# Moving the loads and DMA transposes of six units apart, and the work that waits for them, in a fused retention and MLP kernel

## The chip, the core and the metric

One core of a Trainium2 chip runs the whole kernel. The metric is the device time of one execution in microseconds (us). Engines are named as in the profile: PE is the matrix engine (its weight loads are shown apart as PEld), DVE the vector engine, ACT the scalar engine, POOL the general engine, SP the engine that here only issues DMAs. Each engine runs its own queue of instructions in order, and engines wait for one another with semaphores.

## What is computed

```python
# q, k, v: (8, 8, 576, 64)
scores = scale * np.matmul(q, k.transpose(0, 1, 3, 2))
gamma = 1.0 - 2.0 ** (-5.0 - np.arange(H, dtype=np.float32))
Dmat = np.where(rel >= 0, gamma[:, None, None] ** rel[None, :, :], 0.0)   # rel = i - j
x = np.matmul(scores * Dmat[None], v)       # then heads side by side: 4608 x 512
h = x @ w_in                                # 512 x 2048
out = (h * (1.0 / (1.0 + np.exp(-1.702 * h)))) @ w_out   # 2048 x 512
```

A retention layer (attention without softmax, with a decay that depends on the head) over 8 batches of 576 tokens, and a two-layer MLP with a quick gelu over all 4608 tokens.

## The kernel before

**Units and chunks.** The 4608 tokens are 36 units of 128. Four units are a chunk, and the 9 chunks go through the MLP one after the other. Chunk 0 is units 0 to 3, chunk 1 units 4 to 7, chunk 2 units 8 to 11, and so on. While PE works on the MLP of chunk c, the retention of chunk c + 1 is strewn in between.

**What a unit needs.** `load` issues three DMAs on POOL: k and q into a bf16 tile `kqn` (line 214), v into `vn` (line 227). There are 12 such tiles, so unit 12 uses the tiles of unit 0. Scores need k and q with the head dimension on the partitions. For units 0 to 7 PE transposes them (line 344) and ACT or DVE copies them out of PSUM. From unit 8 on one DMA, issued on SP, transposes `kqn` into `kqT` (`dma_transpose`, line 371). There are 8 tiles `kqT`, with the keys T0 to T7: unit 8 uses T0, unit 13 uses T5.

**Retention in pairs.** Pair j is units 2j and 2j + 1. Unit 8 is one of the units that hold the last 64 tokens of two batches and carry no state on.
- `scale_v` (DVE, line 336) multiplies v with its decay, into `vp`.
- `ahead(j)` puts on PE the scores of the pair (line 477, reading `kqT`) and its contribution to the running state (line 406).
- `ahead_out(j)` puts on DVE the masking of the scores (line 486, into `pm`) and the running sums of the state (lines 419 and 421, into `stm`), and then `state_cast` on ACT, the cast of the sums to bf16 (line 430, into `kv`).
- `block(j)` puts on PE the part that comes from earlier tokens (`inter`, line 461, reading `kv` and `kqT`) and that from the unit itself (`values`, line 499), with `ahead(j + 1)` between two halves of the latter; on DVE it scales the results into `xT` (line 524) and runs `ahead_out(j + 1)`.

**The MLP.** `up` multiplies `xT` with 128 columns of w_in (four matmuls) into PSUM bank A or B by turns, and ACT takes gelu of it into `gT` (line 541). Chunks 0 and 1 do part of it in halves (`up_group`, lines 550 and 555). `down(c, r, s)` multiplies `gT` of unit r of the chunk with w_out, in four quarters s of four matmuls (line 562). `finish_unit` copies the result out (ACT, line 572) and stores it by a DMA on SP (line 578).

**What sets the order.** The order of each engine's queue is the order in which the Python functions call `op`. The class `Program` derives the waits: for each key that an operation reads or writes it waits for the last writer, and for a write also for the readers. A DMA has a semaphore of its own per tile. `load(u, after=[...])` and `dma_transpose` are ordered among one another only through these keys and through their place in POOL's and SP's queue. `lead_in` writes chunk 0, `steady` the others.

Around the change:
- Loads 0 to 11 are issued in `lead_in`. Loads 12 and 13 read key T3, so they wait for the transpose of unit 11.
- Transposes 8 and 9 stand behind the store of the second unit of chunk 0, 10 to 13 behind the fourth.
- The loads of chunk c's far units read the key of the last transpose before them: those of 14 to 17 wait for the transpose of unit 13.
- In chunk 1 the pair of units 8 and 9 has its scores after `up_group` number 11 of 16 and its cast after number 14; `block(4)` stands after down(1, 0, 0), `block(5)` after down(1, 2, 0).

Of the kernel before, what the change touches and what calls it, by code (L numbers as in the profile page):

```python
# [15 lines left out]
NU = (B * S) // P  # L16
# [142 lines left out]
def bass_retnet_parallel__then__act_gelu_quick_kernel(  # L159
# [10 lines left out]
    with es:  # L170
# [195 lines left out]
                transpose_copy(u, 0, bk, ck)  # L366
            transpose_copy(u, 1, bq, cq)

        def dma_transpose(u):
            sl = u % NLD  # L370
            op("sp", lambda e: e.dma_start_transpose(  # L371
                kqT[u % NQT].ap(), kqn[sl].ap().rearrange("p t h d -> p (t h d)")),
               reads=[f"kq{sl}_0", f"kq{sl}_1"], writes=[f"T{u % NQT}_0", f"T{u % NQT}_1"],
               dma=f"d_T{u % NQT}")

        def key(u, a):
# [280 lines left out]
        def lead_in():  # L657
            load_kq0(0)
            load_kq0(1)
            iota_small()  # L660
            iota_large()
            load_v(0)
            load(1)
            load_win(0)
            load(2)
            load_win(1)
            load(3)
            load_win(2)
            load_win(3)
            for i in range(4):  # L670
                load_wout(i)
            for u in range(4, NPE + 4):
                load(u)
            op("dve", lambda e: e.memset(gT[1][:, 0, :], 0.0), writes=["warm"])
            warm(7)
            setup_dve()
            setup_dve2()
            setup_vfac()
            for a in range(4):
                gq_first(a)  # L680
            g_powers()
            gelu_table()
            cast_kq0(0, "dve")
            cast_kq0(1, "dve")
            transpose_pe(0, 0, "E")
            transpose_copy(0, 0, "E", "dve")
            warm(1)
            transpose_pe(0, 1, "B")
            transpose_copy(0, 1, "B", "act")
            warm(4)  # L690
            scores(0)
            scale_v(0)
            gq_next(1)
            scores_out(0, 1, 0)
            scores_out(0, 1, 1)
            state_half(0, 0)
            warm(2)
            transpose_pe(1, 0, "E")
            transpose_copy(1, 0, "E", "act")
            warm(1)  # L700
            transpose_pe(1, 1, "B")
            transpose_copy(1, 1, "B", "act")
            gq_next(2)
            block1(0)
            scale_v(1)
            warm(2)
            scores(1)
            warm(3)
            state_half(1, 0)
            scores_out(1, 1, 0)  # L710
            scores_out(1, 1, 1)
            warm(3)
            block1(1)
            warm(4)
            up_group(0, 0, 2, 0, 2, "A")
            transpose_pe(2, 0, "E")
            transpose_copy(2, 0, "E", "dve")
            up_group(0, 2, 2, 0, 2, "B")
            transpose_pe(2, 1, "E")
            transpose_copy(2, 1, "E", "act")  # L720
            warm(2)
            scale_v(2)
            scores(2)
            state_half(2, 0)
            gq_next(3)
            scores_out(2, 1, 0)
            scores_out(2, 1, 1)
            warm(2)
            up_group(0, 4, 2, 0, 2, "A")
            block1(2)  # L730
            up_group(0, 6, 2, 0, 2, "B")
            transpose_pe(3, 0, "E")
            transpose_copy(3, 0, "E", "dve")
            up_group(0, 0, 4, 2, 3, "A")
            transpose_pe(3, 1, "E")
            transpose_copy(3, 1, "E", "act")
            scale_v(3)
            up_group(0, 4, 4, 2, 3, "B")
            state_half(3, 0)
            scores(3)  # L740
            scores_out(3, 1, 0)
            scores_out(3, 1, 1)
            up_group(0, 8, 2, 0, 2, "A")
            block1(3)
            up_group(0, 10, 2, 0, 2, "B")
            up_group(0, 8, 2, 2, 4, "A")
            up_group(0, 10, 2, 2, 4, "B")
            up_group(0, 0, 4, 3, 4, "A")
            up_group(0, 4, 4, 3, 4, "B")
            gq_next(4)  # L750
            gq_next(5)
            for f in range(12, NF):
                up(0, f)
            def after8():
                ahead(2)
                scores_out(4, 2, 0)
                scores_out(4, 2, 1)

            def after9():
                transposes(6, "B", "B")  # L760
                for u in (4, 5):
                    state_sum(u, 0)
                    state_sum(u, 1)
                scale_v(6)
                scale_v(7)
                state_cast(4, 6)

            work = {
                (0, 3): lambda: (scale_v(4), transposes(4, "E", "E")),
                (1, 3): lambda: (scale_v(5), transposes(5, "C", "C")),  # L770
                (2, 0): after8,
                (2, 1): after9,
                (2, 3): lambda: transposes(7, "C", "C"),
                (3, 0): lambda: block(2, cast=False),
            }
            for r, s in [(i % 2, i // 2) for i in range(8)] + [(i // 4, i % 4) for i in range(8, NF)]:
                down(0, r, s, "AB"[r % 2])
                if (r, s) in work:
                    work[r, s]()
                if s == 3:  # L780
                    finish_unit(0, r, "AB"[r % 2])
                    if r == 1:
                        dma_transpose(8)
                        dma_transpose(9)

        def steady():
            for c in range(1, NCH):
                if c == 1:
                    dma_transpose(10)
                    dma_transpose(11)  # L790
                    for u in (12, 13):
                        load(u, after=["T3_0"])
                for u in range(4 * c + 6, min(4 * c + 10, NU)):
                    if c > 1 or u > 11:
                        dma_transpose(u)
                for u in range(4 * c + 10, 4 * c + 14):
                    load(u, after=[f"T{(4 * c + 9) % NQT}_0"])
                if c == 1:
                    for i in range(16):
                        f0, lo = 2 * (i % 8), 2 * (i // 8)  # L800
                        up_group(1, f0, 2, lo, lo + 2, "AB"[i % 2])
                        if i == 1:
                            state_cast(6, 8)
                        if i == 3:
                            block(3, lambda: None)
                            scale_v(8)
                            scale_v(9)
                        if i == 8:
                            scale_v(10)
                            scale_v(11)  # L810
                        if i == 11:
                            ahead(4)
                            ahead_out(4, False)
                        if i == 14:
                            state_cast(8, 10)
                else:
                    for f in range(NF):
                        up(c, f)
                        if f % 4 == 0:
                            m = 4 * c + 6 + f // 4  # L820
                            if m < NU:
                                scale_v(m)
                if c == NCH - 1:
                    for r in (3, 0, 1):
                        b = "AB"[(r + 1) % 2]
                        for s in range(4):
                            down(c, r, s, b)
                        finish_unit(c, r, b)
                    for n0, b, cp in ((0, "B", "act"), (256, "A", "dve")):
                        for s in range(4):  # L830
                            down(c, 2, s, b, n0, n0 + 256)
                        finish_unit(c, 2, b, n0=n0, n1=n0 + 256, cp=cp)
                    break
                for r in range(4):
                    for s in range(4):
                        down(c, r, s, "AB"[r % 2])
                        if c == 1 and r == 1 and s == 0:
                            scale_v(12)
                            scale_v(13)
                        if s == 0 and r % 2 == 0:  # L840
                            j = 2 * c + 2 + r // 2
                            if 2 * j < NU:
                                block(j)
                    finish_unit(c, r, "AB"[r % 2])

        lead_in()
        steady()
# [60 lines left out]
```

## Time and profile before

| | us |
|---|---|
| median of 3 runs (300.06, 301.92, 302.25) | 301.92 |
| span of the profiled execution | 299.2 |
| POOL idle before the loads of unit 12 | 21.7 |
| first and last issue of a transpose for units 8 to 13 | 49.98, 77 |
| loads of unit 12 issued from | 68.48 |
| loads of unit 14 issued from | 80.83 |
| scores of units 8 and 9 on PE, from | 65.99 |
| block(4) on PE, from | 70.96 |
| block(5) on PE, from | 79.13 |
| PE begins the up projections of chunk 2 | 87.2 |

A line of the profile's table of groups names the line of the code, the engine, the operation, the tile written and the tiles read, the count, the busy time and mean of one, and the idle time of the engine just before with what ended most of it. In a timeline the columns are start, duration, then the same names; a bracket at the end gives the idle time before and what ended it. "issue" there means that the engine waited for nothing that the profile shows. SP's rows are the instructions that issue DMAs, not the transfers; the table of DMA issues gives the time from issue to landing.

### The profile page before, as it was taken

How to read it: one execution, taken by the hardware profiler on the slowest of the kernel's cores; microseconds unless marked ns; L12 is line 12 of the kernel's file. 1: busy time of each engine (PE TensorE's matmuls, PEld its weight loads, DVE VectorE, ACT ScalarE, POOL GpSimd, SP SyncE). 2: the span in 40 equal slices, each digit the busy share in tenths (PEclk: the TensorE clock that was granted, in tenths of full speed). 3: DMA queues.
4: the chain of work that ended last, by engine and by line, in shares of the span. 5: the costliest groups of instructions: out<-in, count | busy, mean ns of one | idle time of the engine just before them, and what ended most of it. 6: DMA issues, size and time to landing. Idle time of an engine off the chain costs nothing.

```text
span 299.2 us, 7913 instructions
## 1 busy us (share of the span) xinstructions
PE 289.9 (97%) x3583; PEld 141.5 (47%) x3583; DVE 98.7 (33%) x198; ACT 135.1 (45%) x236; POOL 108.2 (36%) x137
## 2 busy tenths in 40 slices
PE   7989998989999999999999999999999999999996
PEld 2568354766443454345334443444344534443344
DVE  6553037435541245114800580048005700410000
ACT  8346344653246423642365226522662266216611
POOL 9999482007194085076009500940080000000000
PEclk9999999999999999999999999999999999999999
DMA  9999999999999999999379927991995160110021
GB/s 165 166 209 206 207 219 247 148 161 104 192 169 176 137 110 227 210 112 186 122 175 99 210 58 200 123 195 41 194 103 89 40 142 0 37 72 35 0 71 71
DMA packets 117234, 40.63 MB, mean 136 GB/s; under 512 B 106064, under 2 KB 110416, under 8 KB 117200
## 3 DMA queue, kind: packets, MB, share of 16 engines
q0 software_dynamic: 80160, 22.81, 67.2%
q1 hardware_dynamic: 37040, 17.31, 27.7%
q8 instruction: 28, 0.46, 0.7%
q14 instruction: 6, 0.05, 0.1%
HBM read 36.70 MB, written 9.44 MB: 154 GB/s over the span
## 4 chain that ended last, share of the span: by engine, by line
PE 67%; DMA 15%; POOL 14%; issue 2%; SPq 1%; ACT 0%; DVE 0%; POOLq 0%
PE psA L562 18%; PE psB L562 17%; PE psA L536 14%; PE psB L536 14%; DMA kqn<-in_q_dram 8%; POOL kqn L214 7%; DMA kqT<-kqn 7%; POOL vn L227 4%; POOL w_in_sb L252 2%; PE psX L461 1%; POOL w_out_sb L259 1%; PE psC L477 1%; PE psK L406 1%; PE psX L499 1%; SPq L371 1%
## 5 line engine op out<-in xcount | busy, mean ns | idle before, releaser
L214 POOL DMA_DIRECT2D kqn<-in_k_dram x39 | 35.0, 907 | 113.2 <-DMA kqT<-kqn 110.5
L562 PE MATMUL psA<-w_out_sb,gT 128*128 128x512 bf16 (+1 forms) x304 | 70.3, 374 | 0.0
L562 PE MATMUL psB<-w_out_sb,gT 128*128 128x512 bf16 (+1 forms) x288 | 64.4, 373 | 1.4 <-issue 1.4
L536 PE MATMUL psA<-xT,w_in_sb 128*128 128x512 bf16 x232 | 59.5, 379 | 0.0
L536 PE MATMUL psB<-xT,w_in_sb 128*128 128x512 bf16 x232 | 59.5, 379 | 0.0
L430 ACT ACTIVATE kv<-stm 128x1024 bf16<-128x1024 f32 (+1 forms) x16 | 15.2, 949 | 71.9 <-DVE stm L421 71.9
L524 DVE TENSOR_TENSOR xT<-psX,gq 128x512 bf16<-128x512 f32 x16 | 11.1, 692 | 107.1 <-PE psX L499 107.1
L562 PEld LDWEIGHTS psB<-w_out_sb,gT 128*128 128x128 bf16 x288 | 27.7, 98 | 33.8 <-issue 2.4
L562 PEld LDWEIGHTS psA<-w_out_sb,gT 128*128 128x128 bf16 x304 | 27.6, 98 | 31.3 <-ACT gT L541 2.5
L541 ACT ACTIVATE gT<-psA 128x512 bf16<-128x512 f32 x58 | 34.6, 597 | 15.5 <-PE psA L536 15.5
L541 ACT ACTIVATE gT<-psB 128x512 bf16<-128x512 f32 x58 | 34.6, 597 | 15.4 <-PE psB L536 15.4
L227 POOL DMA_DIRECT2D vn<-in_v_dram x40 | 36.9, 930 | 3.2 <-issue 3.1
L336 DVE TENSOR_TENSOR vp<-vn,vfac 128x512 bf16<-128x512 f32 x36 | 23.7, 687 | 43.4 <-DMA vn<-in_v_dram 43.4
L214 POOL DMA_DIRECT2D kqn<-in_q_dram x39 | 35.3, 917 | 0.0
L536 PEld LDWEIGHTS psA<-xT,w_in_sb 128*128 128x128 bf16 x232 | 18.6, 97 | 31.2 <-ACT gT L541 15.9
L536 PEld LDWEIGHTS psB<-xT,w_in_sb 128*128 128x128 bf16 x232 | 18.0, 97 | 32.1 <-ACT gT L541 15.9
L572 ACT ACTIVATE osb<-psB 128x512 f32<-128x512 f32 (+1 forms) x18 | 10.5, 586 | 20.6 <-PE psB L562 20.6
L550 PE MATMUL psB<-xT,w_in_sb 128*128 128x256 bf16 (+1 forms) x128 | 14.7, 259 | 1.2 <-issue 1.2
L550 PE MATMUL psA<-xT,w_in_sb 128*128 128x256 bf16 (+1 forms) x128 | 14.6, 260 | 0.3 <-DMA w_in_sb<-in_moe_w_in_dram 0.3
L572 ACT ACTIVATE osb<-psA 128x512 f32<-128x512 f32 x18 | 10.5, 584 | 9.6 <-PE psA L562 9.6
L486 DVE TENSOR_TENSOR pm<-psC,mask 128x512 bf16<-128x512 f32 (+1 forms) x20 | 12.6, 630 | 5.0 <-PE psD L477 5.0
L486 DVE TENSOR_TENSOR pm<-psD,mask 128x512 bf16<-128x512 f32 (+1 forms) x20 | 12.6, 628 | 0.0
(67 smaller groups left out, 257.2 us busy)
## 6 DMA issues: line engine op xcount, KB each, us to landing
vn<-in_v_dram POOLq DMA_DIRECT2D x32, 256.0 KB, 5.8
out_dram<-osb SPq DMA_DIRECT2D x31, 256.0 KB, 2.7
kqn<-in_k_dram POOLq DMA_DIRECT2D x31, 128.0 KB, 4.8
kqn<-in_q_dram POOLq DMA_DIRECT2D x31, 128.0 KB, 5.5
w_in_sb<-in_moe_w_in_dram POOLq DMA_DIRECT2D x8, 256.0 KB, 8.9
w_out_sb<-in_moe_w_out_dram POOLq DMA_DIRECT2D x4, 512.0 KB, 16.6
out_dram<-osb SPq DMA_DIRECT2D x10, 128.0 KB, 2.8
vn<-in_v_dram POOLq DMA_DIRECT2D x8, 128.0 KB, 7.1
```

Of the source, the lines that this page charges most:

```text
L214: e.dma_start(kqn[sl][p0 : p0 + n, which, :, :], src[b, :, s0 : s0 + n, :].rearrange("h p d -> p h d"),)
L227: e.dma_start(vn[sl][p0 : p0 + n, :, :], v[b, :, s0 : s0 + n, :].rearrange("h p d -> p h d"))
L252: op("pool", lambda e: [e.dma_start(w_in_sb[64 * pb : 64 * pb + 64, :, 512 * i : 512 * i + 512], moe_w_in[256 * pb : 256 * pb + 256, 512 * ...
L336: op(eng, lambda e: e.tensor_tensor(vp[u % NVP].ap(), vn[sl].ap(), vfac[:, ty, :, None].to_broadcast([P, H, DH]), ALU.mult), reads=[f"vn{s ...
L430: op("act", lambda e: e.activation(kv[:, i0 % NKV : i0 % NKV + n, :, :], stm[:, i0 % 8 : i0 % 8 + n, :, :], AF.Copy), reads=[f"stm{(i0 + i ...
L486: op("dve", lambda e: e.tensor_tensor(pm[(u0 // 2) % 2][hh][:, c0:c1].rearrange("p (a i) -> p a i", i=64), ps32(SB[hh])[:, c0:c1].rearrang ...
L524: op("dve", lambda e: e.tensor_tensor(xT[ch % 2][:, slice(hh, 4, 2), P * jj : P * jj + 2 * P].rearrange("p g (u t) -> p u g t", u=2), ps32 ...
L536: op("pe", lambda e, a=a: e.matmul(bank[b][:, n0:n1], w_in_sb[:, a, P * f : P * f + P], xT[c % 2][:, a, n0:n1], start=(a == 0), stop=(a == ...
L541: op("act", lambda e: e.activation(gT[c % 2][:, f, n0:n1], bank[b][:, n0:n1], AF.Gelu_apprx_sigmoid), reads=[b], writes=[f"g{c % 2}_{f}_{j ...
L550: op("pe", lambda e, a=a, f=f, i=i: e.matmul(bank[b][:, n * i : n * i + n], w_in_sb[:, a, P * f : P * f + P], xT[c % 2][:, a, P * lo : P * ...
L562: op("pe", lambda e, f=f: e.matmul(bank[b][:, 0 : n1 - n0], gT[c % 2][:, f, P * r : P * r + P], w_out_sb[:, f, n0:n1], start=(f == 0), sto ...
L572: op("act", lambda e: e.activation(dst, src, AF.Copy), reads=[b], writes=[f"osb{i}_{n0}"])
```

## The change

Loads 12 and 13 are put right behind load 11, without a wait for a transpose. The six transposes of units 8 to 13 follow on SP, behind the four stores of chunk 0; each reads the key vn1, whose last writer is the load of v of unit 13, so that the first of them waits for it. With this loads and transposes, which were mixed, come in two groups. The loads of units 14 to 17 wait for the transpose of unit 13 as before.

As the transposes come later, what reads them is put later. The scores of units 8 and 9 with all that `ahead_out` has, the cast too, go after down(1, 0, 0). `block(4)` goes after down(1, 1, 0), `block(5)` after down(1, 2, 2). The cast of units 12 and 13 goes from `block(5)` to the end of chunk 1, behind the copy of its last unit. `scale_v` of 12 and 13 keeps its place in the code and comes ahead of `block(4)`'s work on DVE now. The other chunks are as they were.

```diff
-        def dma_transpose(u):
+        def dma_transpose(u, after=()):
...
-               reads=[f"kq{sl}_0", f"kq{sl}_1"], writes=[f"T{u % NQT}_0", f"T{u % NQT}_1"],
+               reads=[f"kq{sl}_0", f"kq{sl}_1", *after], writes=[f"T{u % NQT}_0", f"T{u % NQT}_1"],
...
                     finish_unit(0, r, "AB"[r % 2])
-                    if r == 1:
-                        dma_transpose(8)
-                        dma_transpose(9)
...
                 if c == 1:
-                    dma_transpose(10)
-                    dma_transpose(11)
                     for u in (12, 13):
-                        load(u, after=["T3_0"])
-                for u in range(4 * c + 6, min(4 * c + 10, NU)):
-                    if c > 1 or u > 11:
+                        load(u)
+                    for u in range(8, 14):
+                        dma_transpose(u, ["vn1"])
+                if c > 1:
+                    for u in range(4 * c + 6, min(4 * c + 10, NU)):
                         dma_transpose(u)
...
-                        if i == 11:
-                            ahead(4)
-                            ahead_out(4, False)
-                        if i == 14:
-                            state_cast(8, 10)
...
-                        if s == 0 and r % 2 == 0:
+                        if c == 1 and (r, s) == (0, 0):
+                            ahead(4)
+                            ahead_out(4)
+                        if (r, s) in (((1, 0), (2, 2)) if c == 1 else ((0, 0), (2, 0))):
                             j = 2 * c + 2 + r // 2
                             if 2 * j < NU:
-                                block(j)
+                                block(j, cast=j != 5)
                     finish_unit(c, r, "AB"[r % 2])
+                    if c == 1 and r == 3:
+                        state_cast(12, 14)
```

## The prediction

> **What bounds the kernel now.** I read the page's totals first, then the waits of TensorE (PE) between 40 and 135 us, then the instructions behind them in the timelines of PE, SP, DVE and ACT.
>
> ```profile
> PE 289.9 (97%) x3583; PEld 141.5 (47%) x3583; DVE 98.7 (33%) x198; ACT 135.1 (45%) x236; POOL 108.2 (36%) x137
> ...
> q8 instruction: 28, 0.46, 0.7%
> ```
>
> PE is busy 289.9 of 299.2 us; the other engines are below half. So PE's own order sets the end, and only about 9.3 us of idle PE can be won at all, some 2.7 of them after its last matmul and some 2.7 in the first 20 us, which no edit touches. Who holds PE up in the middle:
>
> ```profile
> PE psB L550 <- issue: 1.2, 1, 1.2
> PE psB L562 <- issue: 0.9, 1, 0.9
> PE psC L477 <- DMA kqT<-kqn: 0.5, 1, 0.5
> PE psC L344 <- DMA kqn<-in_q_dram: 0.3, 1, 0.3
> PE psC L477 <- ACT kqT L354: 0.3, 1, 0.3
> ```
>
> The columns are who waited, for what: us in total, times, longest. Only the third line is a wait for a DMA transpose. The two longest are "issue": nothing in the profile released them. In PE's timeline they, their relative at 145 us and the wait for the transposes are
>
> ```profile
> 51.90 1.25 PE L562 MATMUL psB<-w_out_sb,gT 128*128 128x512 bf16 x5 [0.86 <-issue]
> ...
> 61.75 0.81 PE L550 MATMUL psB<-xT,w_in_sb 128*128 128x256 bf16 x6 [1.25 <-issue]
> ...
> 80.48 0.21 PE L477 MATMUL psC<-kqT 64*64 64x64 bf16 x1 [0.51 <-DMA kqT<-kqn]
> ...
> 145.29 3.19 PE L562 MATMUL psB<-w_out_sb,gT 128*128 128x512 bf16 x14 [0.51 <-issue]
> ```
>
> The view by stretches counts 730 matmuls started before the first "issue" gap, 857 before the second, 2009 before the third. The distances are 127 and 1152 = 9 x 128. The q8 line has 28 packets in 0.46 MB, and 2 x 3583 matmuls and weight loads over 28 packets make 256 instructions, or 128 matmuls, for each. I take these gaps as PE waiting for its next block of instructions, which comes by DMA. That is an inference from the counts. The gap at 61.75 ends 9.9 us after the gap at 51.90, as long as the DMA transposes of that stretch took. In SP's timeline and the table of DMA issues (issues 51.5 to 55.5 us; then 149 to 151 us, where no load is under way):
>
> ```profile
> 49.98 5.37 SPq L371 DMA_TRANSPOSE kqT<-kqn  x2
> ...
> 149.58 5.36 SPq L371 DMA_TRANSPOSE kqT<-kqn  x4
> ```
>
> ```profile
> kqT<-kqn SPq DMA_TRANSPOSE x1, 11.3
> ...
> kqT<-kqn SPq DMA_TRANSPOSE x2, 2.8
> ```
>
> A transpose beside queued loads lands after 11.3 us, one alone after 2.8, and alone they follow one another every 5.36 / 4 = 1.34 us.
>
> **What the skill says.** The Trainium skill, "DMA: Bandwidth & Descriptors", section "Issuing engines are not separate DMA queues", says that DMAs from all issuing engines share 16 DMA engines and interleave. The trace agrees: 11.3 against 2.8 us. Its section "Queues, rings and completion order" says that each DMA engine goes round its queues packet by packet. That fits instructions being late behind transposes; no view shows the order of packets. Its section "Rules for kernel authors" says that a transpose next to ordinary DMAs needs nothing. That is about correctness; in time the neighbourhood costs, as above. No page that I read bears on the wait for PE's instructions.
>
> **The change part by part.**
>
> *Loads 12 and 13 no longer wait for the transpose of 11.* Before, POOL idles 21.7 us and issues them at 68.48. Now they follow load 11, from 46.8 to 52 us. Units land every 2.5 us when little is between them: v of unit 9 at 40.62 + 12.4 = 53.0, of unit 10 at 55.5. Unit 11 came only at 63.8 (DVE's wait for v ends there), with three transposes among the loads. Without them I carry 2.5 us on: unit 11 at 58, 12 at 60.5, 13 at 63. The other bound is 5 us each (the slower steps later in the trace, v of 16 to 17: 96.3 to 102.8, have transposes among them): 70.5. I take 63.5.
>
> *Six transposes behind all loads* (the wait on vn1 is the load of v 13). SP's stores of chunk 0 come before them in its queue and are out by 56.6, and the next store is due only at 78, so nothing else is held on SP. From 63.5 at 1.34 us each and 2.8 us to land: 8 and 9 by 67.7, 10 and 11 by 70.4, 12 and 13 by 73.0. Before, 8 landed at 61.3, 11 at 68.1, 13 at 80.4. The loads of 14 to 17, which wait for 13, start near 73 instead of 80.8.
>
> *Scores of 8 and 9 (ahead(4)) later.* Before they ran at 65.99 to 66.50 inside the up projections; now after the first quarter of down(1,0), at 70.0 + 0.86 - 0.5 = 70.4, or 69.1 if the 1.25 us gap is gone. The transposes are there at 67.7: no wait, margin 1.4. The matmuls are the same ones at another place, and the number of interruptions of the large matmuls is the same: nothing. The cast of unit 9's state has to be ready for block(4). In the trace DVE ends the last sum 2.65 us after the scores begin, and the cast takes 0.62: 73.7 against block(4) at 74.4. Nothing.
>
> *Blocks 4 and 5.* They move from (0,0) and (2,0) to (1,0) and (2,2), six quarters apart instead of eight. In the trace block(4) starts at 70.96 and its cast of two states ends at 77.54, 6.58 us later. The next block comes 1.16 + 6 x 0.863 = 6.34, with the switch some 6.4 us later. So its second group waits **+0.2** us (0 to 0.4).
>
> *Cast of 12 and 13 behind the last copy of chunk 1.* ACT then has the copy, the cast and the first gelu in a row:
>
> ```profile
> 85.36 1.06 ACT L430 ACTIVATE kv<-stm 128x1024 bf16<-128x1024 f32 x1 [6.38 <-DVE stm L421]
> 86.32 0.58 ACT L572 ACTIVATE osb<-psA 128x512 f32<-128x512 f32 x1
> 87.38 0.60 ACT L572 ACTIVATE osb<-psB 128x512 f32<-128x512 f32 x1 [0.48 <-PE psB L562]
> 88.24 0.60 ACT L541 ACTIVATE gT<-psA 128x512 bf16<-128x512 f32 x1 [0.27 <-PE psA L536]
> ```
>
> Copy to cast 0.5, cast to gelu 0.96 (85.36 to 86.32), gelu 0.60: bank A is free 2.1 us after the end of down(1,3). PE wants it for the third up group after 2 x 0.863 = 1.73. **+0.4** us (0 to 0.6), once, as gelu's 0.60 is below the 0.86 of a group.
>
> *What goes.* The wait at 80.48 (0.51) and that for the transpose of unit 17 near 102.7 (0.10): **-0.6**. The gap at 61.75: its instructions were asked for after 51.9, and from there to 63.5 no transpose is under way now. With loads alone in the queue a block needs no more than about 4 us (the gap at 51.9 ended some 4 us after the fast run of small matmuls at 48 us), and there are 9: **-1.25** (0 to -1.4). The gap at 51.9 lies among the same loads; I leave it. The next blocks of instructions come while six transposes run, 63.5 to 73; I add **+0.2** for a late transpose or block (0 to 1.5).
>
> Sum: -0.6 - 1.25 + 0.2 + 0.4 + 0.2 = -1.05. From 301.92 that is **300.9 us**.
>
> **The rivals.** *No gain*, 302.0 us: the gap stays or moves to a block fetched beside the six transposes, so +0.6 stands against -0.6: 301.92 + 0.0 to 0.2. For it: the origin of the gaps is inferred. Against it: both large ones fall where DMA is fullest. *All goes*, 298.7 us: the gaps at 51.9 (0.86) and 145 (0.51) vanish too and the two ACT waits are hidden: 301.92 - 0.61 - 1.25 - 0.86 - 0.51. For it: every later load starts some 7 us earlier, and the runs of before differ by 2.2 us, as waits at the edge would make them. Against it: the first gap precedes the first edit that acts. *A new wait at ahead(4)*, 306 us: the six transposes hang on the last of the loads. At 5 us a unit v 13 lands at 70.5, 9 at 74.7, and PE stands 4.3 us at 70.4 with all down projections behind it in its queue: 301.9 + 4.3 - 0.6 + 0.6 = 306.2. For it: unit 11 took 8.3 us. Against it: that was with transposes among the loads.
>
> **How the numbers follow.** Forecast 0.50, no gain 0.22, all goes 0.18, new wait 0.10. The predicted time is the forecast's, 300.9. The range, 298.8 to 303.3: down nearly to "all goes", up by the bounds of the added waits (1.4 more) and the spread of the three times of before; most of "new wait" is left out. Faster by over 1% (below 298.9) is "all goes" with a little of its misses: 0.17. Slower by over 1% (above 304.9): 0.08. Within: 0.75.
>
> **What would show it.** Right: six transposes 1.34 us apart on SP beginning near 63.5; loads of 14 near 73; no gap of over 0.5 us on PE near 60; no wait for kqT in PE's waits; gelu some 0.4 us late at the start of chunk 2. Wrong: PE waiting at line 477 for kqT near 70 (the transposes are later than I have them), or a gap of "issue" of 1 us at another multiple of 128 matmuls.

## The result: 297.9 us, and where the time went

The changed kernel took **297.9 us** (median of 4 runs, 297.64 to 298.54) against 301.7 us. The ratio is 0.9886, with a 95% interval of 0.9844 to 0.9928. Beside later experiments it was measured twice more: 0.9920 (0.9893 to 0.9947) and 0.9944 (0.9921 to 0.9967). So it is faster by 0.6 to 1.1%, by 2.0 to 3.8 us between the medians, where 1.05 was forecast and 298.8 was the lower end of the range. The kernel before differs more from one set of runs to the next (medians of 300.4 to 301.7 us) than the changed one (297.9 to 298.7), and that makes a good part of the difference between the three ratios.

The page of the changed kernel, the lines that answer to those of before:

```profile
span 295.8 us, 7882 instructions
...
PE 285.1 (96%) x3551; PEld 141.3 (48%) x3583; DVE 97.9 (33%) x198; ACT 135.1 (46%) x236; POOL 108.1 (37%) x137
...
q8 instruction: 28, 0.46, 0.7%
```

The matmuls are the same: 3583 weight loads as before, while 32 records of matmuls are missing from this trace (3551 of 3583). They appear as "issue" waits of 0.16 us and are no gaps. PE's waits between 40 and 135 us, with columns as before:

```profile
PE psA L562 <- issue: 1.0, 6, 0.2
PE psA L536 <- ACT gT L541: 0.4, 1, 0.4
PE psA L562 <- ACT osb L572: 0.4, 1, 0.4
PE psB L562 <- issue: 0.3, 2, 0.2
```

The wait for `kqT` is gone, and so are the gaps of 1.2 and 0.9 us. New is the wait of an up projection for gelu, the second line. SP's timeline has the transposes:

```profile
41.64 11.54 SPq L578 DMA_DIRECT2D out_dram<-osb  x4
63.29 8.55 SPq L371 DMA_TRANSPOSE kqT<-kqn  x6
```

and the table of DMA issues between 63 and 72 us has their time to landing:

```profile
kqT<-kqn SPq DMA_TRANSPOSE x6, 3.1
```

Six transposes from 63.29 on, 8.55 / 6 = 1.43 us each, landing after 3.1 us (median) where those beside loads took 11.3. DVE shows that the loads were early too: its four multiplications of v for units 8 to 11 ran in one go, none waiting for the v of unit 11, which came at 63.8 before.

```profile
57.86 2.49 DVE L336 TENSOR_TENSOR vp<-vn,vfac 128x512 bf16<-128x512 f32 x4
...
70.55 1.28 DVE L336 TENSOR_TENSOR vp<-vn,vfac 128x512 bf16<-128x512 f32 x2
```

**A ledger by stage.** The copies of the results (ACT, line 572) are milestones that both kernels pass in the same order. The table has the time from one to the next, in us, for two traces of the kernel before and three of the changed one.

| stage, from copy to copy | before | before, 2nd | after | after, 2nd | after, 3rd |
|---|---|---|---|---|---|
| start to unit 1 | 42.73 | 42.16 | 42.45 | 42.11 | 43.79 |
| unit 1 to 3 (matmul 730 lies here) | 10.46 | 10.49 | 9.78 | 10.09 | 9.79 |
| unit 3 to 7 (matmul 858, scores and blocks of chunk 1) | 34.19 | 35.73 | 32.13 | 32.33 | 32.14 |
| unit 7 to 11 (late cast, transposes 14 to 17) | 30.29 | 30.88 | 30.61 | 30.61 | 30.62 |
| unit 11 to 15 (matmul 2009) | 30.85 | 30.17 | 30.17 | 30.17 | 30.17 |
| unit 15 to the last | 146.24 | 146.27 | 146.29 | 146.44 | 146.27 |

All the gain lies ahead of unit 15; the last stage differs by no more than 0.2 us. Stage "3 to 7" gives 1.9 to 3.6 us, depending on the pair of traces, and "1 to 3" 0.4 to 0.7. Whether the latter comes from the change is taken up below. The 0.68 us at matmul 2009 is in one trace of before only.

### The profile page after: what moved, and what is told of

Its sections match the earlier page's. It is cut to its first block, busy times and chain, and to the rows that moved or that the text cites. A ratio compares the mean times of both kernels' runs of the same rounds, so it can differ in the third digit from the quotient of the medians.

```text
span 295.8 us, 7882 instructions
## 1 busy us (share of the span) xinstructions
PE 285.1 (96%) x3551; PEld 141.3 (48%) x3583; DVE 97.9 (33%) x198; ACT 135.1 (46%) x236; POOL 108.1 (37%) x137
## 4 chain that ended last, share of the span: by engine, by line
PE 87%; POOL 4%; DMA 3%; ACT 2%; issue 1%; DVE 1%; POOLq 0%; DVEq 0%
PE psA L562 21%; PE psB L562 20%; PE psA L536 17%; PE psB L536 17%; DMA w_in_sb<-in_moe_w_in_dram 3%; PE psA L550 3%; PE psB L550 3%; POOL kqn L214 2%; PE psX L461 2%; POOL vn L227 1%; PE psC L477 1%; POOL w_in_sb L252 1%; PE psX L499 1%; PE psY L499 1%; PE psK L406 1%
## 5 line engine op out<-in xcount | busy, mean ns | idle before, releaser
L214 POOL DMA_DIRECT2D kqn<-in_k_dram x39 | 35.6, 921 | 110.6 <-DMA kqT<-kqn 107.8
L562 PE MATMUL psA<-w_out_sb,gT 128*128 128x512 bf16 (+1 forms) x287 | 66.6, 373 | 2.8 <-issue 2.4
L562 PE MATMUL psB<-w_out_sb,gT 128*128 128x512 bf16 (+1 forms) x285 | 63.7, 373 | 0.5 <-issue 0.3
L562 PEld LDWEIGHTS psB<-w_out_sb,gT 128*128 128x128 bf16 x288 | 27.8, 98 | 32.1 <-issue 0.6
L536 PEld LDWEIGHTS psB<-xT,w_in_sb 128*128 128x128 bf16 x232 | 18.1, 97 | 32.0 <-ACT gT L541 15.5
```

The costliest lines, as they stand in the source:

```text
L214: e.dma_start(kqn[sl][p0 : p0 + n, which, :, :], src[b, :, s0 : s0 + n, :].rearrange("h p d -> p h d"),)
L536: op("pe", lambda e, a=a: e.matmul(bank[b][:, n0:n1], w_in_sb[:, a, P * f : P * f + P], xT[c % 2][:, a, n0:n1], start=(a == 0), stop=(a == ...
L562: op("pe", lambda e, f=f: e.matmul(bank[b][:, 0 : n1 - n0], gT[c % 2][:, f, P * r : P * r + P], w_out_sb[:, f, n0:n1], start=(f == 0), sto ...
```

## The experiments

Theory A: transposes and loads in flight together slow each other, and with them the DMA that brings PE's next block of instructions; keeping them apart brings the gain. Theory B: the gain comes from PE's new order, or from the early loads as such. Theory C: the "issue" gaps have nothing to do with instructions.

### Only the DMAs changed

Loads and transposes as in the changed kernel, the order of PE, DVE and ACT as before.

```diff
-                    if r == 1:
-                        dma_transpose(8)
-                        dma_transpose(9)
...
-                    dma_transpose(10)
-                    dma_transpose(11)
                     for u in (12, 13):
-                        load(u, after=["T3_0"])
+                        load(u)
+                    for u in range(8, 14):
+                        dma_transpose(u, ["vn1"])
```

> Loads 12 and 13 early and the six transposes behind them, but PE's, DVE's and ACT's order as before. Theory A (PE's blocks of 128 matmuls come late when transposes and loads are mixed): the gap at matmul 857 is gone and the one at 730 is half, some 2.1 us won by 61 us, and the wait for the transpose of 12 (0.5) is gone; but PE now reaches the scores of 8 and 9 near 63.7 us while their transposes land near 66 and 67.5, so it waits some 3 to 3.5 us at line 477 for kqT. About 301.5 us, the gain spent in that wait. Theory B (the gain is from waits that the new order of PE avoids, the gaps are chance): gap at 857 still there, PE reaches the scores near 66 and waits 1 to 1.5 us; about 302.5 us.

Ratio 1.0074 (1.0043 to 1.0105): slower than before. The gap at 858 is gone, and PE stands at the scores of units 8 and 9, in its timeline:

```profile
67.33 0.21 PE L477 MATMUL psC<-kqT 64*64 64x64 bf16 x1 [3.62 <-DMA kqT<-kqn]
68.69 0.26 PE L477 MATMUL psC<-kqT 64*64 64x64 bf16 x1 [1.04 <-DMA kqT<-kqn]
```

That is 4.7 us of waiting, where A had 3 to 3.5, since the transposes began at 64.46 in this run. The waits also cost clock: the page's PEclk row falls to 7 in one slice after them. So this separation of all six gives nothing without the later scores.

### Only PE's order changed

The DMAs as before, the rest as in the changed kernel.

```diff
+                    if r == 1:
+                        dma_transpose(8)
+                        dma_transpose(9)
...
+                    dma_transpose(10)
+                    dma_transpose(11)
                     for u in (12, 13):
-                        load(u)
-                    for u in range(8, 14):
-                        dma_transpose(u, ["vn1"])
+                        load(u, after=["T3_0"])
+                    dma_transpose(12)
+                    dma_transpose(13)
```

> The DMAs in the order of before (transposes 8 to 11 among the loads, loads 12 and 13 after the transpose of 11), PE, DVE and ACT in the new order. Theory A: gaps of 0.9 us or more at matmuls 730 and 857 stay, the wait for the transpose of 12 goes (-0.5), the late cast costs +0.5: about 301.7 us, the same as before. Theory B: most of the gain is here, 298 to 299 us.

Ratio 1.0155 (1.0088 to 1.0223): slower by more than either theory had. Neither had seen why. `scale_v` of 12 and 13 now stands ahead of block(4)'s work on DVE, and there it waits for loads that are still late. DVE's timeline:

```profile
75.15 0.69 DVE L336 TENSOR_TENSOR vp<-vn,vfac 128x512 bf16<-128x512 f32 x1 [3.02 <-DMA vn<-in_v_dram]
77.52 0.69 DVE L336 TENSOR_TENSOR vp<-vn,vfac 128x512 bf16<-128x512 f32 x1 [1.68 <-DMA vn<-in_v_dram]
78.12 0.68 DVE L524 TENSOR_TENSOR xT<-psX,gq 128x512 bf16<-128x512 f32 x1
```

PE's timeline then has

```profile
83.45 0.21 PE L461 MATMUL psX<-kqT,kv 64*64 64x64 bf16 x1 [2.91 <-ACT kv L430]
```

All that block(4) has on DVE comes behind v 13, so the sums and the cast do, and block(5) stands 2.9 us. So the first half of B is refuted: PE's order brings nothing by itself, and it needs the early loads.

### Without the gate on v 13

```diff
-                        dma_transpose(u, ["vn1"])
+                        dma_transpose(u)
```

> The changed kernel without the wait of the transposes on the load of v 13: they go as soon as the k and q of their own unit are there, so 8, 9, 10 run from about 53 us beside the loads of 11 to 13. Theory A: the gap at matmul 857 comes back with about 1.2 us, the one at 730, which lies before the first transpose, stays at about 0.6: about 299.1 us. Theory B: what counts is that the loads start early, so 297.9 us as in the changed kernel.

Ratio 1.0013 (0.9990 to 1.0036): the whole gain is lost through this one wait less. The early loads and PE's new order are both still there, so the second half of B is refuted too. A had the sign, and the wrong place: no gap came back at 858. PE ran the scores of unit 8 at 67.34 without a wait and then stood at those of unit 9, whose transpose had not landed. PE's timeline:

```profile
71.48 0.26 PE L477 MATMUL psC<-kqT 64*64 64x64 bf16 x1 [3.83 <-DMA kqT<-kqn]
```

The view of busy times by stretch (PE, PEld, DVE, ACT, POOL, then clock, DMA share, GB/s):

```profile
65.00:70.00 5.00, 2.60 (x34) 1.58 (x32) 0.00 (x0) 1.62 (x3) 0.00 (x0) 0.96 1.65 90
70.00:75.00 5.00, 3.18 (x38) 1.55 (x40) 2.65 (x5) 0.63 (x1) 0.00 (x0) 0.50 1.40 117
75.00:80.00 5.00, 4.60 (x133) 2.51 (x133) 1.25 (x2) 0.60 (x1) 0.09 (x1) 0.86 1.20 182
```

The transpose of 9 was issued at 54.29, 10.4 us earlier than in the changed kernel (64.73), and landed at 71.44, 4.0 us later (67.48). After the wait PE ran at a clock of 0.50. At 0.96, 0.50 and 0.86 the three stretches lose 3.4 us of clock, some 0.9 of them while PE waited anyway. 3.8 + 2.5 = 6.3 us, and the span is 302.0 against 295.8. This loss of clock belongs to the traced run, which at 303.78 us is the longest of 20. In 13 of them the clock stayed at 1.00, and the median, 301.95, lies 3 to 4 us above the medians of the changed kernel, about the length of the one wait.

### The gaps moved by 24 matmuls

The kernel before with 24 extra small matmuls at the head of PE's queue. They change nothing in the output.

```diff
             warm(7)
+            for _ in range(24):
+                op("pe", lambda e: e.matmul(
+                    bank["A"][0:64, 0:64], gT[1][0:64, 0, 0:64], gT[1][0:64, 0, 0:64], skip_group_check=True),
+                   reads=["warm"], writes=["A"])
```

> The kernel before with 24 more small matmuls (64x64, result not used) on PE right after its first warm-up matmuls. Theory A (blocks of instructions): the gaps stay at matmul counts of about 730, 857 and 2009 with the 24 counted, so they move 24 matmuls earlier in the program; the second is then at a small matmul or an up group before the one of the kernel before; about 302 us and up to 1 us more, as PE runs faster into the second. Theory C (the gaps belong to a place in the program, a wait that the profile does not show): they stay at the same instructions, at counts 754, 881 and 2033.

Ratio 1.0070 (1.0040 to 1.0101). PE's timeline has the two gaps at other instructions:

```profile
50.23 0.21 PE L406 MATMUL psE<-vp,kqn 64*64 64x64 bf16 x1 [1.34 <-issue]
...
60.59 0.81 PE L550 MATMUL psA<-xT,w_in_sb 128*128 128x256 bf16 x6 [2.59 <-issue]
```

Before they stood at a down and at an up group in bank B; now at a state matmul and at an up group in bank A, and again 730 and 858 weight loads lie ahead of them (858 is the gap that the prediction has at 857, counted there by matmuls). So the gaps keep to PE's count: C is refuted, and the blocks of 128 matmuls are shown. The second grew from 1.25 to 2.59, in the main as PE was there some 0.8 us earlier. The traced run took 301.98 us, near the 302 that A had; the median of all 20 is 305.36, and no trace shows what the longer ones waited for.

The trace has the packets of the q8 queue, each 16384 bytes, 28 in all. I set the end of the last DMA packet to the end of the span and took the end of the sixth packet, the one for matmul 858, from the moment when PE went on with the block before, at matmul 730. This makes the packets 0.9 us later than the times that they have in the trace, and that is too much: in the changed kernel the 1024th packet of the transposes, with which that of unit 8 is through, then starts at 66.51, while unit 8 landed at 66.12. So the figures serve to compare kernels, and each is 0.4 us or more too large (0.9 if the trace's own times hold):

```text
kernel                         transposes 8, 9 issued near 50 us   packet has come after
before, 1st / 2nd                          yes                          8.6 / 9.0 us
before + 24 matmuls                        yes                          8.8
only PE's order changed                    yes                          7.4
changed, 8 and 9 early                     yes                          7.8
changed, 1st / 2nd / 3rd                   no                           6.3 / 6.4 / 6.1
only the DMAs changed                      no                           6.3
no gate (first transpose 52.7)             no                           6.3
two rounds, PE before / changed            no                           6.2 / 6.0
cast on DVE                                no                           6.1
```

PE reaches matmul 858 some 8.3 us after it went on at 730 in these kernels (7.5 with the 24 more). Where the packet took 6.0 to 6.4 us, or 7.4 and 7.8, there is no gap; where it took 8.6 to 9.0 there is one. All five traces with early transposes have it later than all eight without. The fifth packet fits as well: in all 13 traces, the changed kernel's too, PE's weight loads pause after the first 730 (for 0.6 to 1.5 us) and go on some 0.4 to 0.65 us after the end of that packet on this scale.

### Two of the six transposes back among the loads

The changed kernel with the transposes of 8 and 9 at their old place.

```diff
+                    if r == 1:
+                        dma_transpose(8)
+                        dma_transpose(9)
...
-                    for u in range(8, 14):
+                    for u in range(10, 14):
                         dma_transpose(u, ["vn1"])
```

> The changed kernel with the transposes of 8 and 9 alone put back among the loads, at their old place on SP (about 50 and 54 us), the other four still behind the load of v 13. Theory A: their landing takes 11 us again, 61 and 65 us, well before PE wants them at 67.7, so no wait for them; but the gap at 730 grows from 0.64 to 1.2 us or so and that at 857 comes back with 0.5 to 1.3: 298.8 to 299.8 us. Rival (only the late transposes of 12 and 13 mattered, the gaps are not from transposes beside loads): 297.9 us.

Ratio 1.0021 (0.9992 to 1.0049): all of the gain lost again, more than A had, and the gap at 858 not back (the packet took 7.8 us). What A had overlooked is the other direction. DVE's timeline has the loads:

```profile
65.25 0.69 DVE L336 TENSOR_TENSOR vp<-vn,vfac 128x512 bf16<-128x512 f32 x1 [5.00 <-DMA vn<-in_v_dram]
```

v 11 comes at 65.2 where the changed kernel's fourth multiplication ran by 59.7 without a wait, and SP starts the four gated transposes at 71.5 in place of 63.3 to 64.6 (three traces). Two transposes cost the loads 7 to 8 us, and PE waits 1.21 and 1.04 us for the transposes of 10 and 11. Counting the trace's DMA packets shows how much each kind gets through. The stretches, at the times that the packets have in the trace, are such that one of the two kinds is under way alone, or both throughout (the first has some packets of stores as well):

```text
                          128-byte packets    256-byte packets     GB/s,
                          of loads, per us    of transposes        all DMAs
changed, 51 to 60 us            708                   0              247
changed, 65 to 69 us              0                 748              192
before, 55 to 59 us             110                 276              121
two early, 54 to 58 us          220                 227              126
two early, 59.5 to 63.5 us      258                 237              122
no gate, 58 to 67 us            197                 200              103
```

The view of busy times by stretch has the last column at the end of its lines, for the loads alone, the transposes alone and "no gate":

```profile
51.00:60.00 9.00, 8.91 (x133) 6.85 (x133) 5.68 (x12) 5.50 (x9) 0.31 (x1) 1.00 1.86 247
65.00:69.00 4.00, 3.79 (x74) 2.63 (x74) 0.52 (x1) 1.99 (x4) 0.00 (x0) 1.00 0.85 192
58.00:67.00 9.00, 8.95 (x81) 7.08 (x80) 1.71 (x3) 6.24 (x11) 0.00 (x0) 1.00 1.63 103
```

Measured by what each does alone, the mixtures do 15.5 + 36.9 = 52%, 61%, 68% and 55%. So mixing loses a third to a half of the DMA's work, and the transposes get 27 to 37% of their rate. In "no gate" as many packets of the one kind as of the other get through, 197 and 200 per us. A packet of a transpose took 18 ns alone and 67 ns on average there, one of a load 32 and 48. (In "before" few loads were left at that time.)

### Apart, but in two rounds

Here the transposes of 8 to 11 wait for v 11, and the loads of 12 and 13 wait for the transpose of 11 as before: separation in the first round without early loads. Once with PE's order of before, once with the changed one.

```diff
-                    if r == 1:
-                        dma_transpose(8)
-                        dma_transpose(9)
...
-                    dma_transpose(10)
-                    dma_transpose(11)
+                    for u in range(8, 12):
+                        dma_transpose(u, ["vn11"])
                     for u in (12, 13):
                         load(u, after=["T3_0"])
```

> The kernel before with one thing changed: the transposes of 8 to 11 wait for the load of v 11, so no transpose runs beside the loads of 8 to 11. Loads 12 and 13 stay behind the transpose of 11, PE's order stays. If transposes beside loads are the cause (each kind slows the other): v 11 lands near 58.5 in place of 64, the four transposes by 65.5 in place of 68, loads 12 and 13 are issued near 65.7 in place of 69, no gap at matmul 857, no wait for the scores of 8 (PE there at 63.7, landing 61.5), a wait of 0 to 0.8 us for the transposes of 12 and 13, no cost of the late cast: 297.5 to 298.3 us. If the early loads and the new order on PE are what brings the gain: 300 to 301 us, as before.

> The changed kernel with the DMAs in two rounds: loads to 11, transposes 8 to 11 behind the load of v 11, loads 12 and 13 behind the transpose of 11, then transposes 12 and 13. PE's order as in the changed kernel. If the separation is the cause and not that loads 12 and 13 are issued early: 298 us as in the changed kernel, with 12 and 13 landing near 76 and no wait at block(5), but DVE's scale_v of 12 and 13, which stands ahead of block(4)'s work on DVE, may wait some us for v 13 and hold up the cast that block(5) needs, by 0 to 2 us. If the early loads are the cause: 300 us or more.

With the order of before the ratio is 0.9970 (0.9945 to 0.9996): a little faster, with no gap at 858, but between the two expectations and short of the changed kernel's 0.9944 (0.9921 to 0.9967) on the same chip (medians of 22 runs each: 299.78 and 298.70 us). What is left are waits for transposes in PE's timeline:

```profile
65.68 0.21 PE L477 MATMUL psC<-kqT 64*64 64x64 bf16 x1 [0.41 <-DMA kqT<-kqn]
...
80.35 0.21 PE L477 MATMUL psC<-kqT 64*64 64x64 bf16 x1 [0.70 <-DMA kqT<-kqn]
...
103.05 0.21 PE L477 MATMUL psC<-kqT 64*64 64x64 bf16 x1 [0.59 <-DMA kqT<-kqn]
```

Those at 80 and 103 are the chain that hangs on the loads of 12 and 13, issued at 67.77 here. In stage "3 to 7" this kernel takes 33.68 us, half way between before (34.19 and 35.73) and after (32.1 to 32.3). So the first separation carries a small part alone. The rest came with the early loads and PE's later order together; what each of these two does for it isn't separated here. With PE's changed order the ratio is 1.0136 (1.0077 to 1.0196): `scale_v` waits for v 13 until 78.5, and block(5) 3.8 us for the cast, as in "only PE's order changed". I had allowed 2.

### The late cast, and second traces

```diff
-                        state_cast(12, 14)
+                        op("dve", lambda e: e.tensor_copy(
+                            kv[:, 24 % NKV : 24 % NKV + 4, :, :], stm[:, 0:4, :, :]),
+                           reads=[f"stm{i}" for i in range(4)], writes=[f"kv{(24 + i) % NKV}" for i in range(4)])
```

> The changed kernel with the cast of the states of 12 and 13 as one copy on DVE right behind its sums, in place of ACT's cast at the end of chunk 1. If that cast costs PE the 0.4 to 0.6 us that the trace shows before the third up group of chunk 2, 297.4 us, and that gap is gone; if the gap has another cause, 297.9 us.

ACT's timeline of the changed kernel shows copy, cast and gelu in a row:

```profile
84.36 0.60 ACT L572 ACTIVATE osb<-psB 128x512 f32<-128x512 f32 x1 [2.86 <-PE psB L562]
84.86 1.05 ACT L430 ACTIVATE kv<-stm 128x1024 bf16<-128x1024 f32 x1
85.80 0.59 ACT L541 ACTIVATE gT<-psA 128x512 bf16<-128x512 f32 x1
```

and PE's the wait that comes of it:

```profile
86.45 1.04 PE L536 MATMUL psA<-xT,w_in_sb 128*128 128x512 bf16 x4 [0.40 <-ACT gT L541]
```

The gelu at 85.80 ends at 86.39, and PE's third up group, which takes the same bank, goes on at 86.45. With the cast on DVE that wait is gone, and stage "7 to 8" (last copy of chunk 1 to first of chunk 2) is 21.03 us where three traces of the changed kernel have 21.59 or 21.60. The ratio is 0.9913 (0.9881 to 0.9945), the changed kernel's beside it 0.9920. The half microsecond is in the traces; in the whole time it can't be told from the changed kernel.

The kernels themselves once more:

> The kernel before once more, for a second trace. Theory A (blocks of 128 matmuls that come late when transposes run beside loads): gaps at the same counts, 730 and 857, of about 1 us each but not of the same length, since it depends on the packets. Rival (chance): gaps elsewhere or none.

> The changed kernel once more, beside the experiments of this call. All theories: 297.9 us, and the PE gaps of its first trace again (about 0.6 us on the weight loads at matmul 730, none of 0.5 us or more at 857 and 2009, 0.4 us before the third up group of chunk 2).

> The changed kernel beside the two others on the same chip: 0.989 to 0.992 of the kernel before. All theories.

The second trace of before has gaps at the same counts and more waiting for transposes than the first, in PE's timeline:

```profile
51.36 1.25 PE L562 MATMUL psB<-w_out_sb,gT 128*128 128x512 bf16 x5 [0.89 <-issue]
...
61.49 0.81 PE L550 MATMUL psB<-xT,w_in_sb 128*128 128x256 bf16 x6 [1.53 <-issue]
...
80.49 0.21 PE L477 MATMUL psC<-kqT 64*64 64x64 bf16 x1 [1.05 <-DMA kqT<-kqn]
81.48 0.21 PE L477 MATMUL psC<-kqT 64*64 64x64 bf16 x1 [0.67 <-DMA kqT<-kqn]
...
104.18 0.21 PE L477 MATMUL psC<-kqT 64*64 64x64 bf16 x1 [0.59 <-DMA kqT<-kqn]
```

2.3 us for transposes, where the first trace had 0.6. In no trace of the changed kernel does PE wait for one. The third set of the changed kernel, 0.9944, gained less than the 0.989 to 0.992 that was expected.

## Why the prediction was wrong

The mechanism was right and the sum was too small: 1.05 us forecast, 2.0 to 3.8 measured; 297.9 lay below the range and nearest to the rival "all goes" (298.7). All five signs named for being right came: the six transposes from 63.29 on, the loads of 14 at 73.90, no gap near 60, no wait for `kqT`, the late gelu. The steps that failed are the size of "What goes", which was read from one trace, and two of the added costs, which did not come. Step by step:

- **"What goes": the waits for transposes, -0.6.** The mechanism was right, the term mis-sized. The first trace of before has 0.51 + 0.10, the second 2.3 (the wait near 102.7 is for unit 15, which landed at 102.65, not for unit 17). The wait hangs on the end of a DMA chain that runs close to when PE needs it, so one trace is one draw. The times said so: the profiled run of before took 300.97, the median 301.92, and the sum left this 0.95 us out.
- **The gap at matmul 858, -1.25.** Right: 1.25 and 1.53 in two traces of before, none in three of after, with a packet of instructions that came after 6.1 to 6.4 us in place of 8.6 to 9.0. That no transpose may run beside it was right too. The working had too much room: it gave a block about 4 us beside loads alone, counted from 51.9, and 6.1 to 6.4 were measured from there.
- **"The gap at 51.9 lies among the same loads; I leave it."** Put at nothing, while stage "1 to 3" shrank by 0.4 to 0.7 us between these traces. That the change did this is not shown. In before the first packet of a transpose moves at 53.5 us or later in both traces, when that gap is over. And the stage is short (9.99 and 9.98 us) in "only PE's order changed" and in "two of the six", where transposes 8 and 9 are issued at the old place, as it is in "only the DMAs changed" and in "no gate" (9.79 and 9.71); it stayed long in the second kernel of two rounds (10.55, a gap of 0.91), with no transpose before 59. The cause stays open.
- **The gap at 145 us.** Left out of the forecast, and 0.68 us of the first pair of traces; but it is absent from the second trace of before, so it is a draw too.
- **The added costs, +0.8.** The late cast cost 0.40 in PE's wait, as worked out, and 0.56 by the stage "7 to 8". The cast for block(5) and the late transpose or block, +0.2 each, did not show: stage "3 to 7" shrank by 2.06 where 1.25 + 0.51 was to go.
- **Landing times.** v 13 was put at 63.5 and the six transposes began at 63.29; 13 was put at 73.0, and the loads of 14, which wait for it, were issued at 73.90 (75.4 and 77.1 in the other two traces). The margin at ahead(4) held in all three traces.

Against the rival "a new wait at ahead(4)", the gate on v 13 turned out to prevent just that wait: without it PE stands 3.8 us there.

The Trainium skill, "DMA: Bandwidth & Descriptors", section "Rules for kernel authors", has it that a transpose next to ordinary DMAs needs nothing. In time two transposes cost the loads 7 to 8 us here, and beside loads the transposes lost 63 to 73% of their rate.

## What to carry to other kernels

A gate that makes a transfer start later can make it land sooner, and everything behind it as well, where two kinds of DMA slow each other: look at landing times, not issue times. Such a gate, the early loads and the later readers had their full worth only together: the DMAs alone moved the wait to PE's scores, the order alone to DVE and the cast, and a gate for four transposes alone won 0.3%. And when the engine that bounds a kernel waits at the end of a DMA chain, one trace shows one draw of that wait; take the spread of the times as part of what the change can win.

## What was not expected of the hardware

- PE's instructions come in blocks of 128 matmuls with their weight loads, 16384 bytes each, over the DMA engines. The block for matmul 858 came 6.0 to 6.4 us after PE went on at 730 with loads alone in flight, and 7.4 to 9.0 us with transposes too, on the scale above.
- Transposes beside loads ran at 200 to 276 packets per us against 748 alone, the loads at 110 to 258 against 708.
- A wait of 2.9 to 3.8 us on PE cost clock as well: in four traces the clock was 0.50 for 3.4 us ("only PE's order changed", "only the DMAs changed") or 6.8 us ("no gate", the second kernel of two rounds). The Trainium skill, "TensorE: Matmul & The Clock Gate", section "HAM oscillation — how this bites in real kernels", says that PE gaps above some 3.4 us throttle it again; here a wait of 2.91 us ("only PE's order changed") was followed by it, and in "no gate" the clock fell 1.9 us into the wait. A wait of 2.6 us ("24 matmuls") left the clock at 1.00 in its trace.
